# Moving one of four startup transposes from the matrix engine to VectorE, with a new block-0 schedule, a later bias transpose and a two-piece last split

## The chip, the cores and the metric

The kernel runs on one core of one Trainium2 chip. The metric is the time of one execution in device microseconds; lower is better. PE is the matrix engine (PEld its weight loads), DVE is VectorE, ACT is ScalarE, POOL is GpSimd and SP issues the DMAs. "Sub-tile j" is the j-th group of 128 tokens of a 512-token block; "f-tile" is a slice of 128 of the 3584 hidden features. In this kernel SBUF holds the tiles that the engines work on and PSUM the results of PE.

## The reference

```python
# B, S, D, F = 1, 2048, 1024, 3584, all bf16
def reference(x, w1, b1, w2, b2):
    y = _layernorm(x, axis=-1)                       # no scale, no shift, eps 1e-5
    h = _gelu(jnp.einsum("bsd,df->bsf", y, w1) + b1) # tanh approximation
    return jnp.einsum("bsf,fd->bsd", h, w2) + b2
```

## The kernel before

The tokens are taken in four blocks of 512 (four sub-tiles each). For every block PE computes `w1.T @ yT` per f-tile into one of four PSUM banks `pa`, ScalarE applies bias and GELU into `hT`, and then PE multiplies `hT` with `w2` into two banks `pb`, from which VectorE adds `b2` and writes the output tile. PE needs the normalised tokens transposed (`yT`).

For blocks 1 to 3 VectorE does that transpose in SBUF, far ahead of need. For block 0 nothing is ahead: PE transposes all four sub-tiles into PSUM (`pt`), ScalarE copies the first two to `yT`, VectorE the last two. So that PE can begin early, block 0 is computed in pieces, as sub-tiles become ready. The configuration says so:

```python
n_warm=12, n_fill=(2, 0, 0, 0),
# (first f-tile, end, first sub-tile, end)
sched0=((0, 2, 0, 1), (0, 2, 1, 2), (2, 4, 0, 2), (0, 4, 2, 3), (4, 8, 0, 3), (8, None, 0, 4), (0, 8, 3, 4)),
tpos=(0, 0, 5, 9),      # before which group PE transposes sub-tile j
edve=(2, 3),            # sub-tiles that VectorE copies out of PSUM
dve0=(("Sa", 0), ("Sb", 0), ("Sa", 1), ("Sb", 1), ("N", 0), ("N", 1), ("Sa", 2), ("Sb", 2),
      ("Sa", 3), ("N", 2), ("Sb", 3), ("E", 2), ("N", 3), ("E", 3)),   # VectorE's order in block 0
b1pos=0,                # PE transposes the bias row before the first group
last_split=(256, 128, 128),
```

`Sa` and `Sb` are statistics of the two halves of a sub-tile (they wait for its load), `N` the normalisation, `E` the copy from PSUM. The two ways to transpose are:

```python
def dve_transposes(t):                   # VectorE, SBUF to SBUF, blocks 1 to 3
    ...
    for si in range(4):
        for dj in range(4):              # 16 instructions of 32 x 256
            ...
            op("dve", lambda e, src=src, dst=dst: e.transpose(dst, src), ...)

def pe_transposes(j):                    # PE, block 0
    ...
    for dt in range(KD):                 # 8 of 128 x 128
        op("pe", lambda e, j=j, dt=dt: e.transpose(pt[tbank[j]][:, dt, :],
                                                   xs[j][:, dt * P:(dt + 1) * P], ident[:]), ...)

for b in range(NB):                      # PE's order
    for gi, (ft, j0, j1) in enumerate(groups[b]):
        if b == 0:
            for j in range(NJ):
                if tpos[j] == gi and j not in dtr0:
                    pe_transposes(j)
                    ...
            if b1pos == gi:
                pe_b1()
        pe_group(b, gi, ft, j0, j1)      # 8 matmuls of 128*(j1-j0) columns
    ...                                  # then the w2 matmuls of this block
```

## Time and profile before

| | before |
|---|---|
| median of the first 4 runs (later 13 runs) | 401.59 us (401.71 us) |
| span of the profiled run | 400.0 us |
| PE busy | 98% of the span |
| PE in the chain of work that ended last | 97% |
| 512-column matmul to the next | 215.8 ns |

The 215.8 ns are 10.79 us per 50 matmuls in the chain. The Trainium skill, "TensorE: Matmul & The Clock Gate", section Back-to-back issue gap, gives N/2.4 + 2.5 ns for warm matmuls, which is 215.8 ns for N = 512: this trace agrees. The kernel needs the equivalent of 1792 such matmuls, 386.7 us. What can be gained lies in the first 16 us, in the last 3 us, and in PE work that is no needed matmul.

Start of the kernel before, in the chain of waits (the chain that ended last, in order of time; columns: start in us, length in us, engine, tile, source line). Line 452 is PE's transposes, 471 the first matmul, 438 the bias transpose:

```profile
8.43 0.62 PE pt L452 x8
9.05 0.12 PE pb L438
9.17 2.93 PE pa L471 x40
12.10 0.45 PE pt L452 x8
12.55 2.30 PE pa L471 x32
14.85 0.45 PE pt L452 x8
15.29 5.65 PE pa L471 x40
...
397.65 0.29 DVE osb L341
```

The transposes of sub-tile 2 stand at 12.10 us and those of sub-tile 3 at 14.85 us. Each eight take 0.45 us and there is PE work directly before and after them, so they are on the critical path. The last line is the last output addition.

VectorE in the same stretch, in the timeline (start, length, line, operation, `[idle before, and what ended it]`):

```profile
13.66 0.55 DVE L311 TENSOR_SCALAR xs<-xs,mv,rs 128x1024 bf16<-128x1024 bf16 x1 [0.38 <-POOL rs L296]
15.33 0.69 DVE L346 COPY yT<-pt 128x1024 bf16<-128x1024 bf16 x1 [1.12 <-PE pt L452]
15.94 0.68 DVE L300 BATCH_NORM_STATS2 st<-xs 128x6 f32<-128x512 bf16 x1
...
20.63 7.18 DVE L328 STREAM_TRANSPOSE yT<-xs 32x256 bf16<-32x256 bf16 x16
```

The first line is sub-tile 3's normalisation, the second the copy of its transposed form out of PSUM. The last line is what the VectorE way of transposing one sub-tile costs: 7.18 us for 16 instructions, here in block 1.

The end of the kernel, in the timeline. The gap between the starts of two additions is the time of the 28 matmuls between them:

```profile
391.47 0.69 DVE L341 TENSOR_TENSOR osb<-pb,b_bc 128x512 bf16<-128x512 f32 x1 [5.35 <-PE pb L491]
...
394.52 0.42 DVE L341 TENSOR_TENSOR osb<-pb,b_bc 128x256 bf16<-128x256 f32 x1 [2.36 <-PE pb L491]
396.09 0.29 DVE L341 TENSOR_TENSOR osb<-pb,b_bc 128x128 bf16<-128x128 f32 x1 [1.14 <-PE pb L491]
397.65 0.29 DVE L341 TENSOR_TENSOR osb<-pb,b_bc 128x128 bf16<-128x128 f32 x1 [1.27 <-PE pb L491]
```

### The profile page before, as it was taken

What the parts mean: (1) busy time and instruction counts of PE and PEld (TensorE: products, weight loads), DVE (VectorE), ACT (ScalarE), POOL (GpSimd) and SP (SyncE); (2) the same over time, 40 slices, a digit from 0 to 9 for tenths busy, and PEclk for the clock granted to TensorE, in tenths of its full rate; (3) what the DMA queues carried; (4) which work ended last, traced back from release to release, by engine and by line L of the source; (5) the groups of instructions that cost most, each with busy time, mean ns of one, the idle gap of its engine ahead of it and who ended that gap; (6) DMA issues with size and microseconds to landing.
All of it is one profiled execution on the core that took longest, in us unless ns stands there. A gap on an engine that the chain in (4) does not pass through costs nothing.

```text
span 400.0 us, 4581 instructions
## 1 busy us (share of the span) xinstructions
PE 393.5 (98%) x1972; PEld 187.6 (47%) x2007; DVE 138.0 (35%) x292; ACT 83.9 (21%) x131; POOL 15.7 (4%) x41
## 2 busy tenths in 40 slices
PE   7999999999999999999999999999999999999997
PEld 3744464444444444444444444444444444444446
DVE  5699930110399940101159991001100000001101
ACT  3533450000033442000023344100003334400000
POOL 3211000000011000000010000000000000000000
DMA  8999940000000000000000000000000000000000
GB/s 245 369 387 386 387 147 13 28 13 26 28 0 2 0 1 2 26 13 28 24 15 2 0 0 2 0 28 26 13 28 13 0 2 0 0 15 26 15 26 27
DMA packets 17486, 23.62 MB, mean 59 GB/s; under 512 B 1339, under 2 KB 9787, under 8 KB 17467
## 3 DMA queue, kind: packets, MB, share of 16 engines
q1 hardware_dynamic: 17466, 23.34, 16.7%
q8 instruction: 15, 0.25, 0.3%
q14 instruction: 5, 0.03, 0.0%
HBM read 19.14 MB, written 4.19 MB: 58 GB/s over the span
## 4 chain that ended last, share of the span: by engine, by line
PE 97%; DMA 1%; DVE 1%; issue 1%; POOL 0%; SPq 0%
PE pa L471 48%; PE pb L491 48%; DMA xs<-in_x_dram 1%; PE pt L452 0%; SPq L252 0%; DVE st L300 0%; DVE st L304 0%; POOL rs L296 0%; DVE xs L311 0%; POOL ve L293 0%; DVE osb L341 0%; DVE mv L306 0%; PE pb L438 0%
## 5 line engine op out<-in xcount | busy, mean ns | idle before, releaser
L471 PE MATMUL pa<-yT,w_sb 128*128 128x512 bf16 (+3 forms) x992 | 194.1, 355 | 0.8
L491 PE MATMUL pb<-w_sb,hT 128*128 128x512 bf16 (+2 forms) x933 | 193.0, 366 | 1.0
L471 PEld LDWEIGHTS pa<-yT,w_sb 128*128 128x128 bf16 x1008 | 93.2, 98 | 100.8 <-DVE yT L346 0.2
L491 PEld LDWEIGHTS pb<-w_sb,hT 128*128 128x128 bf16 x952 | 90.8, 98 | 102.7
L415 ACT ACTIVATE hT<-pa,b_sb 128x512 bf16<-128x512 f32 (+3 forms) x126 | 80.3, 640 | 259.4 <-PE pa L471 258.5
L341 DVE TENSOR_TENSOR osb<-pb,b_bc 128x512 bf16<-128x512 f32 (+2 forms) x34 | 22.4, 660 | 248.3 <-PE pb L491 248.3
L328 DVE STREAM_TRANSPOSE yT<-xs 32x256 bf16<-32x256 bf16 x192 | 83.7, 436 | 2.9
L293 POOL TENSOR_SCALAR ve<-mv 128x1 f32<-128x1 f32 x16 | 5.3, 334 | 209.5 <-DVE mv L306 209.5
L300 DVE BATCH_NORM_STATS2 st<-xs 128x6 f32<-128x512 bf16 x16 | 11.0, 685 | 5.8 <-DMA xs<-in_x_dram 5.6
L304 DVE BATCH_NORM_STATS2 st<-xs 128x6 f32<-128x512 bf16 x16 | 10.8, 677 | 0.0
L296 POOL TENSOR_TENSOR rs<-ve,mhalf 128x1 f32<-128x1 f32 x16 | 9.1, 568 | 1.3
L311 DVE TENSOR_SCALAR xs<-xs,mv,rs 128x1024 bf16<-128x1024 bf16 x16 | 8.2, 513 | 1.3 <-POOL rs L296 1.2
L433 PE MATMUL pb<-zeros 128*128 128x512 bf16 x14 | 5.7, 584 | 1.4 <-POOL scr L283 1.4
L433 PEld LDWEIGHTS pb<-zeros 128*128 128x128 bf16 x14 | 1.8, 137 | 4.1 <-issue 2.8
L306 DVE BATCH_NORM_AGGREGATE mv<-st 128x2 f32<-128x12 f32 x16 | 3.3, 209 | 0.6
L452 PE MATMUL pt<-ident,xs 128*128 128x128 bf16 x32 | 2.5, 220 | 0.9 <-DVE xs L311 0.9
L403 ACT COPY yT<-pt 128x1024 bf16<-128x1024 bf16 x2 | 2.0, 1012 | 5.8 <-PE pt L452 5.8
L452 PEld LDWEIGHTS pt<-ident,xs 128*128 128x128 bf16 x32 | 1.9, 98 | 2.2 <-DVE xs L311 2.1
L346 DVE COPY yT<-pt 128x1024 bf16<-128x1024 bf16 x2 | 1.4, 690 | 1.1 <-PE pt L452 1.1
L399 ACT ACT_TABLE_LOAD x1 | 1.3, 1283 | 0.8 <-PEq L562 0.8
L282 POOL MEMSET zeros<- 128x512 bf16 x1 | 0.5, 524 | 0.3 <-POOLq L562 0.3
L286 POOL TENSOR_SCALAR_AFFINE_SELECT ident<-ones 128x128 bf16<-128x128 bf16 x1 | 0.3, 292 | 0.1
(11 smaller groups left out, 1.5 us busy)
## 6 DMA issues: line engine op xcount, KB each, us to landing
w_sb<-in_w_dram SPq DMA_DIRECT2D x9, 1024.0 KB, 14.4
w_sb<-in_w_dram SPq DMA_DIRECT2D x2, 2048.0 KB, 14.1
out_dram<-osb SPq DMA_DIRECT2D x31, 128.0 KB, 1.7
xs<-in_x_dram SPq DMA_DIRECT2D x15, 256.0 KB, 10.2
w_sb<-in_w_dram SPq DMA_DIRECT2D x2, 512.0 KB, 5.1
xs<-in_x_dram SPq DMA_DIRECT2D x2, 128.0 KB, 2.1
b_bc<-in_b_dram SPq DMA_DIRECT2D x1, 256.0 KB, 10.1
out_dram<-osb SPq DMA_DIRECT2D x1, 64.0 KB, 1.6
```

The costliest lines, as they stand in the source:

```text
L293: lambda e, t=t: e.tensor_scalar(ve[:, t:t + 1], mv[:, t, 1:2], EPS, None, ALU.add),
L296: lambda e, t=t: e.tensor_tensor(rs[:, t:t + 1], ve[:, t:t + 1], mhalf[:], ALU.pow),
L300: op("dve", lambda e, t=t: e.bn_stats(st[:, t, 0:6], xs[t][:, 0:512]), waits=[xev[(t, 0)]], meta=("bnst", 512))
L304: op("dve", lambda e, t=t: e.bn_stats(st[:, t, 6:12], xs[t][:, 512:1024]), waits=[xev[(t, 1)]], sig=("bs", t), ctr="bs", meta=("bnst", 512))
L311: lambda e, t=t: e.tensor_scalar(xs[t][:], xs[t][:], mv[:, t, 0:1], rs[:, t:t + 1], ALU.subtract, ALU.mult),
L328: op("dve", lambda e, src=src, dst=dst: e.transpose(dst, src), waits=waits if k == 0 else (), sig=("yT", t) if last else None, ctr="dt", m ...
L341: lambda e, slot=slot, gi=gi, c0=c0, c1=c1: e.tensor_tensor(osb[slot][:, c0:c1], pb[gi % NBK][:, 0:c1 - c0], b2_bc[:, c0:c1], ALU.add),
L415: lambda e, ft=ft, tok=tok, n=n, bank=bank: e.activation(hT[:, ft, tok], pa[bank][:, 0:n], ACT.Gelu_apprx_tanh, bias=b1_sb[:, ft:ft + 1], ...
L433: lambda e: e.matmul(pb[1][:], lhsT=zeros[:, 0:P], rhs=zeros[:], start=True, stop=True),
L452: lambda e, j=j, dt=dt: e.transpose(pt[tbank[j]][:, dt, :], xs[j][:, dt * P:(dt + 1) * P], ident[:]),
L471: lambda e, b=b, ft=ft, dt=dt, tok=tok, n=n, bank=bank: e.matmul(pa[bank][:, 0:n], lhsT=w1_sb[:, dt, ft * P:(ft + 1) * P], rhs=yT[b % 2][: ...
L491: lambda e, ft=ft, j=j, c0=c0, c1=c1, gi=gi: e.matmul(pb[gi % NBK][:, 0:c1 - c0], lhsT=hT[:, ft, j * P:(j + 1) * P], rhs=w2_sb[:, ft, c0:c ...
```

## The change

The intent is to take eight transposes off PE, which is always busy, and give them to VectorE, which is busy 35% of the time. VectorE is slower at it, so block 0 needs sub-tile 3 one f-tile later (9 instead of 8). Besides, the bias transpose moves behind two groups, the last output tile is split in two pieces instead of three, and the block's end loses the option that spared GpSimd its drain. The rest of the diff turns the configuration into constants and removes unused bookkeeping; the order and sizes of the loads stay.

```diff
-    sched0=((0, 2, 0, 1), (0, 2, 1, 2), (2, 4, 0, 2), (0, 4, 2, 3), (4, 8, 0, 3), (8, None, 0, 4),
-            (0, 8, 3, 4)),
-    tpos=(0, 0, 5, 9),
-    edve=(2, 3),
-    dtr0=(),
-    dve0=(... ("Sa", 3), ("N", 2), ("Sb", 3), ("E", 2), ("N", 3), ("E", 3)),
-    b1pos=0,
-    last_split=(256, 128, 128),
+SCHED0 = ((0, 2, 0, 1), (0, 2, 1, 2), (2, 4, 0, 2), (0, 4, 2, 3), (4, 9, 0, 3), (9, None, 0, 4),
+          (0, 9, 3, 4))
+TPOS = (0, 0, 5)
+B1POS = 2
+DVE0 = (... ("Sa", 3), ("N", 2), ("Sb", 3), ("E", 2), ("N", 3), ("D", 3))   # D: 16 VectorE transposes
+LAST_SPLIT = (384, 128)
 ...  (cut: constants in place of the configuration, bookkeeping)
-        block = es.enter_context(nc.Block(no_gpsimd_drain=True))
+        block = es.enter_context(nc.Block())
```

## The prediction

> **What bounds the kernel.** The matrix engine. The page gives PE 98% busy and the chain of waits is 97% PE. From 9 us to 397.65 us it is all but never idle: the waits view lists 0.9 us for normalised x and 1.4 us at the very start. A 512-column matmul follows the next at 215.8 ns (10.79 us per 50 in the chain), as the Trainium skill, "TensorE: Matmul & The Clock Gate", Back-to-back issue gap, gives with N/2.4 + 2.5 ns; 1792 such equivalents are 386.7 us of a 400.0 us span. Only the first 16 us, the last 3 us and PE work that is not a needed matmul can be saved.
>
> **What the change does, by parts.**
> 1. Eight PE transposes of sub-tile 3 go. In the chain they take 0.45 us (14.85 to 15.29), with no PE wait on either side. Saved: 0.45 us, all on the critical path.
> 2. In place of one 0.69 us copy from PSUM, VectorE does 16 transposes of 0.435 us: 7.18 us in block 1's timeline. The normalisation of sub-tile 3 starts at 13.66 us, so they should run from 14.24 to about 21.42 us. Block-0 work that needs sub-tile 3 starts one f-tile later (9 instead of 8): the PE has five 384-column groups of 1.30 us, to about 21.65 us. Slack only 0.1 to 0.2 us, but both sides hang on the same arrival of x sub-tile 3, so it should hold. I expect a wait of 0 to 0.1 us.
> 3. One 512-column group becomes 384 + 128: same columns, 8 more matmuls of about 2.5 ns fixed cost: +0.02 us.
> 4. The bias transpose (0.12 us in the chain) moves behind the two groups of sub-tile 0. Before, the PE waits about 0.27 us for sub-tile 1's copy on ScalarE (the weight load at 10.16 us was released by it), so the 0.12 us was hidden: saving about 0. The bias copy starts 0.1 us later; four PSUM banks cover it.
> 5. Last split 256+128+128 becomes 384+128: 28 fewer matmuls; 3.05 + 1.57 us become an estimated 4.55: -0.07 us. The last piece, its 0.29 us addition and its store stay.
> 6. At the block's end GpSimd gets a drain and the other engines' drains merge with a semaphore instruction. GpSimd is idle from about halfway. Estimated 0 to -0.05 us.
> 7. Block-1 layernorm on VectorE starts at about 21.4 instead of 15.9 us and ends near 58 instead of 54 us. The first output addition is wanted at about 65 us and block 1's yT at 107 us: nothing waits.
>
> Sum: -0.45 - 0.07 + 0.02 - 0.02 + up to 0.1 = about -0.5 us of 401.6, 0.12%. **Predicted 401.1 us, 8 in 10 between 400.6 and 401.7; faster by over 2%: 0.01; within 2%: 0.98; slower by over 2%: 0.01.**
>
> **What would show it.** (1) 24 PE transposes instead of 32; no transpose piece near 14.9 us in the chain. (2) In the VectorE timeline a 16-transpose run of 7.2 us right after the fourth normalisation, ending near 21.4 us; at most a small new PE wait for yT from the transpose line. (4) The first sub-tile-1 matmul stays near 10.2 us. (5) A 384-wide addition, its matmuls ending 4.55 us after the piece before. (7) No new wait of additions or block 1.
>
> **What would make it wrong.** VectorE transposes slower while DMA writes at 385 GB/s and PE reads the same tile, so that the first full-width group waits up to a microsecond: the gain vanishes. Weights of f-tiles 4 to 8 needed 0.45 us earlier and not landed. A drain on GpSimd that takes microseconds. Execution spread (401.27 to 402.02) exceeds the whole effect.

## The result, and the profile after

| | before | after |
|---|---|---|
| median | 401.71 us (401.27 to 402.19, 13 runs) | 401.47 us (401.05 to 402.20, 9 runs) |
| ratio | | 0.9996, interval 0.9986 to 1.0005 |
| span of the profiled run | 400.0 us | 399.5 us |
| end of sub-tile 2's PE transposes (chain) | 12.55 us | 12.67 us |
| start of the last addition (chain) | 397.65 us | 397.28 us |
| between these two | 385.10 us | 384.61 us |

A ratio is the mean time of one kernel's fast runs over that of the other's of the same rounds, so it is not quite the ratio of the medians quoted.

By the clock the two are the same within noise, as predicted; the medians differ by 0.24 us. The prediction's 401.1 us was 0.37 us too low, inside its range; 0.12 us of that lies in the base, as the prediction started from the 401.59 us of four runs and all thirteen have 401.71 us. The range also holds the 401.59 us of no change at all, so lying in it shows little by itself. The result's list of runs holds a tenth fast run of after, 400.65 us, which the nine of its median leave out; with it the median would be 401.38 us. The trace sees more than the clock can: counted from the end of sub-tile 2's transposes, the rest of the kernel is 385.10 - 384.61 = 0.49 us shorter.

The chain after the change, at the same place (line 412 is PE's transposes, 429 the first matmul, 374 ScalarE's copy of sub-tile 1):

```profile
8.56 0.64 PE pt L412 x8
9.19 0.02 issue
9.21 1.02 ACT yT L374
10.24 0.05 issue
10.28 1.94 PE pa L429 x24
12.22 0.45 PE pt L412 x8
12.67 9.25 PE pa L429 x80
...
397.28 0.29 DVE osb L336
```

There is no transpose piece near 14.9 us, and after 12.67 us the list of waits names no further wait of PE. The bias transpose has left the chain: at this place in this run PE waits for ScalarE's copy of sub-tile 1, which is what covered the bias transpose before.

VectorE after the change:

```profile
13.32 0.55 DVE L303 TENSOR_SCALAR xs<-xs,mv,rs 128x1024 bf16<-128x1024 bf16 x1
13.90 7.18 DVE L319 STREAM_TRANSPOSE yT<-xs 32x256 bf16<-32x256 bf16 x16
21.11 0.69 DVE L292 BATCH_NORM_STATS2 st<-xs 128x6 f32<-128x512 bf16 x1
```

The 16 transposes run at once after the normalisation, take the same 7.18 us as in block 1, and end at 21.08 us. The loads run at 376 GB/s meanwhile, and ran at 387 GB/s during those of block 1 in before; the 16 that start at 208.09 us in before, when the loads are over (8 GB/s from 200 to 220 us), take 7.18 us too. The list of waits names no PE wait for them.

And the end:

```profile
391.17 0.69 DVE L336 TENSOR_TENSOR osb<-pb,b_bc 128x512 bf16<-128x512 f32 x1 [5.35 <-PE pb L448]
...
395.72 0.56 DVE L336 TENSOR_TENSOR osb<-pb,b_bc 128x384 bf16<-128x384 f32 x1 [3.86 <-PE pb L448]
397.28 0.29 DVE L336 TENSOR_TENSOR osb<-pb,b_bc 128x128 bf16<-128x128 f32 x1 [1.01 <-PE pb L448]
```

The 384-column piece takes 395.72 - 391.17 = 4.55 us, against 396.09 - 391.47 = 4.62 us for the 256 and the 128 before.

Two questions stayed. Is the 0.49 us really the sum of the named parts? And why did the clock show only half of it: did something give it back, or is it noise?

### The profile page after: what moved, and what is told of

Same layout as the page of the kernel before. It is cut to its first block, busy times and chain, and to the rows that moved or that the text cites. A ratio compares the mean times of both kernels' runs of the same rounds, so it can differ in the third digit from the quotient of the medians.

```text
span 399.5 us, 4536 instructions
## 1 busy us (share of the span) xinstructions
PE 393.1 (98%) x1944; PEld 186.1 (47%) x1979; DVE 144.2 (36%) x306; ACT 84.3 (21%) x132; POOL 15.6 (4%) x41
## 4 chain that ended last, share of the span: by engine, by line
PE 97%; DMA 1%; issue 1%; DVE 1%; ACT 0%; POOL 0%; SPq 0%
PE pb L448 48%; PE pa L429 48%; DMA xs<-in_x_dram 1%; PE pt L412 0%; ACT yT L374 0%; SPq L245 0%; DVE st L292 0%; DVE st L296 0%; POOL rs L288 0%; DVE xs L303 0%; POOL ve L285 0%; DVE osb L336 0%; DVE mv L298 0%
## 5 line engine op out<-in xcount | busy, mean ns | idle before, releaser
L448 PEld LDWEIGHTS pb<-w_sb,hT 128*128 128x128 bf16 x924 | 89.3, 98 | 104.2
L319 DVE STREAM_TRANSPOSE yT<-xs 32x256 bf16<-32x256 bf16 x208 | 90.7, 436 | 3.1
```

Source lines behind the costliest of these rows:

```text
L448: lambda e, ft=ft, j=j, c0=c0, c1=c1, gi=gi: e.matmul(pb[gi % NBK][:, 0:c1 - c0], lhsT=hT[:, ft, j * P:(j + 1) * P], rhs=w2_sb[:, ft, c0:c ...
```

## The experiments

The yardstick below is the one of the table: from the end of sub-tile 2's PE transposes to the start of the last addition, called *the stream*. It leaves out the start, which differs from execution to execution. The start is told by when these transposes end, called *the start*. Both are read from the chain or, where the chain ran through another engine, from PE's timeline.

| run | start, us | last addition, us | stream, us | median, this / before, us | ratio (interval) |
|---|---|---|---|---|---|
| before | 12.55 | 397.65 | 385.10 | | |
| after | 12.67 | 397.28 | 384.61 | 401.47 / 401.71 | 0.9996 (0.9986 to 1.0005) |
| e1 after again | 12.08 | 396.69 | 384.61 | 401.07 / 401.55 | 0.9984 (0.9969 to 0.9999) |
| e2 after, old block end | 12.14 | 396.75 | 384.61 | 401.05 / 401.55 | 0.9987 (0.9969 to 1.0005) |
| e3 before, new block end | 13.04 | 398.14 | 385.10 | 401.28 / 401.55 | 0.9987 (0.9971 to 1.0004) |
| e4 before, transposes moved | 12.81 | 397.49 | 384.68 | 401.23 / 401.55 | 0.9987 (0.9972 to 1.0002) |
| e5 after, split at 8 | 12.07 | 397.52 | 385.45 | 402.14 / 401.32 | 1.0015 (1.0000 to 1.0031) |
| e6 before, 128 more transposes | 12.17 | 404.42 | 392.25 | 408.55 / 401.32 | 1.0175 (1.0161 to 1.0188) |
| e7 after, VectorE reordered, split at 11 | 12.49 | 397.13 | 384.64 | 400.91 / 401.32 | 0.9987 (0.9974 to 0.9999) |
| e8 after, VectorE reordered | 12.31 | 397.23 | 384.92 | 400.98 / 401.32 | 0.9989 (0.9976 to 1.0001) |
| e9 after, bias late, old place | 13.07 | 397.68 | 384.61 | 401.88 / 401.49 | 1.0005 (0.9990 to 1.0020) |
| e10 after, bias late, new place | 12.25 | 396.86 | 384.61 | 401.15 / 401.49 | 0.9989 (0.9972 to 1.0005) |
| e11 after, old last split | 12.08 | 396.76 | 384.68 | 400.95 (one run) / 401.49 | |
| e12 after, old block end, again | 12.09 | 396.70 | 384.61 | 401.12 / 401.42 | 0.9992 (0.9978 to 1.0006) |

The stream repeats to the hundredth of a microsecond between executions that have the same PE work, while the start moves by a microsecond. That is what makes effects of 0.07 us readable here, where the clock's interval is some 0.4 to 0.7 us to either side.

This yardstick was chosen after the first four runs. The expectations of e1 and e4 name another, from the second x tile's first statistics to the last addition, which takes in part of the loads: it is 392.53 us in before, 392.04 in after and 392.14 in e1 (recorded there as "about 390.0"), but 393.72 in e3, which has the same PE work as before, and 392.91 in e4. By it the expectation of e4 was missed; e3 shows that it does not measure the change.

### e1, e2, e3: is the gain given back at the block's end?

The profiled run of after took 401.67 us with a span of 399.5 us, before took 401.86 us with 400.0 us: 0.3 us more outside of the span. The drain on GpSimd, new at the block's end, was the suspect (theory B); theory A is that only noise hides the gain.

e1 is the changed kernel unaltered.

> The changed kernel once more. Theory A (the change takes 0.5 us of PE work out of the span and the medians differ by less only because executions spread over 1 us): median 0.3 to 0.7 us below the kernel before of the same rounds; in the trace the last addition again starts about 390.0 us after the second x tile's first statistics (392.53 before, 392.04 in the profile of after). Theory B (the span gains 0.5 us but the tail outside of the span gives 0.2 to 0.3 us back, because of the drain on GpSimd): median only 0.1 to 0.3 us below, and time minus span again near 2.1 us against 1.86 us before.

e2 takes the drain from the changed kernel, e3 gives it to the kernel before:

```diff
# e2
-        block = es.enter_context(nc.Block())
+        block = es.enter_context(nc.Block(no_gpsimd_drain=True))
# e3: the reverse, in the kernel before
```

> The changed kernel with the old block end (no drain on GpSimd). Theory A: the same as e1 within 0.1 us, time minus span unchanged. Theory B: 0.2 to 0.3 us faster than e1, so about 0.5 us below the kernel before, and time minus span back near 1.86 us.

> The kernel before with only the new block end (drain on GpSimd, the other engines' drain merged). Theory A: same as the kernel before within 0.1 us. Theory B: 0.2 to 0.3 us slower than the kernel before, the span itself unchanged.

e1 came out 0.48 us below before and e2 0.50 us: no gain from taking the drain away that the clock can see. It cannot see much: e3, which saves no PE work, has the same ratio, 0.9987, as e2 and e4, so the ratios do not show the saving. What decides is time minus span. e1 has 2.08 us and e2 1.90 us in the median, as theory B expects, but e2's six runs scatter from 1.67 to 2.14 us; and e3, the drain alone, has 1.83 us against 1.85 us for before, where B asked for 0.2 to 0.3 us more. So the drain alone costs no time that shows, and theory B in this form falls. In the span the new block end even saves a little: from the start of the last addition to the end of the span it is 2.22 us in e1 and in after, 2.23 us in e3, but 2.32 us in before and 2.30 us in e2. The trace shows why it can: there the separate drain and semaphore instruction of SP at the end are one.

The time outside of the span is taken up again under e12.

### e4: the move of the transposes alone

```diff
# in the kernel before
-    sched0=(... (4, 8, 0, 3), (8, None, 0, 4), (0, 8, 3, 4)),   edve=(2, 3), dtr0=(),   ... ("E", 3)),
+    sched0=(... (4, 9, 0, 3), (9, None, 0, 4), (0, 9, 3, 4)),   edve=(2,), dtr0=(3,),   ... ("D", 3)),
```

> The kernel before with only the move of sub-tile 3's transposes to VectorE and the 9-instead-of-8 schedule. Theory A: 0.43 us less from the second x tile's first statistics to the last addition (392.53 us before), no PE wait for the VectorE transposes, median 0.2 to 0.7 us below before. Rival C (VectorE transposes come too late and PE waits): interval shortened by less than 0.2 us and a wait of PE for yT from the transpose line of some tenths of a us near 21 us.

The chain, with the end of sub-tile 2's transposes and the last addition:

```profile
12.19 0.62 PE pt L452 x8
12.81 11.19 PE pa L471 x89
...
397.49 0.29 DVE osb L341
```

The stream is 384.68 us: 385.10 - 384.68 = 0.42 us shorter, and there is no PE wait for VectorE's transposes. The move alone is thus 0.42 of the 0.49 us. In this run x sub-tile 3 came late and the transposes ended only at 21.74 us (started 14.56 us, 7.18 us long); PE still did not wait. Rival C (they come too late and PE waits) falls.

### e5: is the new schedule needed for it?

```diff
# in the changed kernel
-SCHED0 = (... (4, 9, 0, 3), (9, None, 0, 4), (0, 9, 3, 4))
+SCHED0 = (... (4, 8, 0, 3), (8, None, 0, 4), (0, 8, 3, 4))
```

> The changed kernel with the block-0 schedule split at f-tile 8 as before, sub-tile 3 still transposed on VectorE. Theory A (VectorE's 7.18 us of transposes just fit behind five 384-column groups): with four of them the PE is ready 1.30 us earlier, the transposes are not, so a PE wait for yT of 0.4 to 1.2 us near 20 to 21 us; from the end of sub-tile 2's PE transposes to the last addition 385.0 to 385.8 us instead of 384.61, which is about or worse than the kernel before (385.10). Rival C (the retune of the schedule is idle): no such wait, 384.6 us.

The stream became 385.45 us, 0.84 us longer than with the split at 9, and longer than before. The list of waits of e5 names the reason (columns: engine, tile and line, what it waited for, us in total, times, longest):

```profile
PE pa L429 <- DVE yT L319: 0.7, 1, 0.7
```

Line 319 is the VectorE transposes. The timeline shows PE starting on the first full-width group only as they end:

```profile
13.46 7.18 DVE L319 STREAM_TRANSPOSE yT<-xs 32x256 bf16<-32x256 bf16 x16
...
20.70 9.67 PE L429 MATMUL pa<-yT,w_sb 128*128 128x512 bf16 x44 [0.68 <-DVE yT L319]
```

The idle time listed is 0.68 us, the stream grew by 0.84. The other 0.16 us fits how the idle time is counted, from the modelled end of the matmul before: at the start of this stream the next matmul starts at 11.91 us, 0.16 us before the modelled end of the transposes at 12.07 us.

By the clock the kernel is just slower than before (402.14 against 401.32 us, ratio 1.0015, 1.0000 to 1.0031). The one f-tile more is 1.30 us of PE work; in this run 0.84 us of it was needed. The move and the split at 9 belong together: the move without the later split costs more than it brings.

### e6: what one PE transpose costs

```diff
# in the kernel before, pe_transposes
-        for dt in range(KD):
+        reps = 17 if j == 3 else 1
+        for k in range(reps * KD):
+            dt = k % KD
```

The waits stand at the first and the signal at the last of them, and the result is unchanged.

> The kernel before with sub-tile 3's eight PE transposes done 17 times over (128 more, same result). If one costs 56 ns in the stream as the chain says: 7.15 us more, time about 408.7 us, ratio about 1.018. If a PE transpose costs the 220 ns that the page gives as its mean duration: 28 us more, about 430 us.

The stream grew by 392.25 - 385.10 = 7.15 us for 128 transposes, 55.9 ns each, and the median by 7.2 us. In the chain all 136 stand in one piece:

```profile
12.17 2.30 PE pa L473 x32
14.47 7.59 PE pt L454 x136
22.06 2.07 PE pa L473 x18
...
404.42 0.29 DVE osb L341
```

So the eight that the change removed were worth 8 x 55.9 = 447 ns. The profile page's group of PE transposes, in before, shows a mean of 220 ns; the Trainium skill, "Perfetto Trace Analysis", section Tensor Engine Instruction, says that PE's end times are estimated from size plus a delay rather than observed. This run agrees: spacing, not the mean length, is the cost.

### e7, e8: is it VectorE's queue order that makes the start vary?

In e3 and e4 sub-tile 2's normalisation stood behind sub-tile 3's first statistics, which waited for x sub-tile 3 until 11.23 and 10.99 us, and PE idled 0.35 and 0.63 us. Theory D was that this order makes the start vary; rival E that the first loads alone do.

```diff
# e7, in the changed kernel; with SCHED0 split at 11 instead of 9
-        ("Sa", 3), ("N", 2), ("Sb", 3), ("E", 2), ("N", 3), ("D", 3))
+        ("N", 2), ("E", 2), ("Sa", 3), ("Sb", 3), ("N", 3), ("D", 3))
# e8, split left at 9
+        ("N", 2), ("Sa", 3), ("Sb", 3), ("E", 2), ("N", 3), ("D", 3))
```

> The changed kernel with VectorE's queue reordered: sub-tile 2 is normalised and copied out of PSUM before sub-tile 3's first statistics, which wait for a load (split at f-tile 11, as sub-tile 3 then comes about 1 us later). Theory D (runs differ because the normalisation of sub-tile 2 stands in VectorE's queue behind statistics that wait for x sub-tile 3): the PE's transposes of sub-tile 2 end at 11.6 to 12.0 us from the span's start instead of 12.1 to 13.0 us, span medians 0.2 to 0.6 us below the changed kernel's 399.0, no new PE wait for sub-tile 3. Rival E (the landing of the first x tiles alone sets it): no gain, median again near 401.1 to 401.5 us.

> The changed kernel with sub-tile 2's normalisation alone put before sub-tile 3's first statistics. Theory D: transposes of sub-tile 2 earlier in runs in which x sub-tile 3 lands late, but its copy out of PSUM still behind sub-tile 3's statistics, so PE waits for that copy instead: 0 to 0.3 us gained. Rival E: no gain. The VectorE transposes then end later by up to 0.7 us, and a PE wait for them of 0 to 0.5 us may appear.

Both miss their main expectation. The start in e7 was 12.49 us, not 11.6 to 12.0 us, and the median span is 399.0 us, the same as e1's. The chain of e7 shows why this run started late: x sub-tile 1 landed at 5.06 us (4.55 us or earlier in e1), and statistics, normalisation, PE transpose and ScalarE's copy of sub-tile 1 follow one another from there to 10.05 us. Here, as rival E has it, sub-tile 1's load set the start. The chains of e3 and e4 run as theory D says, from x sub-tile 3's load through its statistics to sub-tile 2's normalisation; that the new order helps in such an execution no run shows, and it is no general gain. e8's stream is 0.31 us longer than after's, and PE waits for sub-tile 2's copy there (0.22 us idle in its timeline), as expected. Against before, the ratios of e7 and e8 (0.9987 and 0.9989) are about those of e1 and e2, so neither is shown to beat the changed kernel.

### e9, e10: what the bias transpose's new place is for

In e3's profile PE waited at the old place: the list of waits names the bias row's load. (The wait did not set the start there: the chain of e3 runs through x sub-tile 3, which landed at 11.20 us.)

```profile
PE pb L438 <- DMA b1row<-in_b_dram: 0.8, 1, 0.8
```

To see this on purpose, the load of the bias row was put one load later, with the transpose in the old place (e9) and in the new one (e10):

```diff
# both, in the changed kernel
-LOADS = (... ("x", 2), ("b1",), ("w1", 2, 4), ("x", 3), ...
+LOADS = (... ("x", 2), ("w1", 2, 4), ("b1",), ("x", 3), ...
# e9 only
-B1POS = 2
+B1POS = 0
```

> The changed kernel with the bias row's load issued one load later (behind the second piece of w1) and the bias transpose put back in front of the first matmul group. Theory F (the old place makes the first matmul wait for the bias row when it lands late): PE waits 0.5 to 1.5 us for the bias row, the first matmul of sub-tile 0 starts at 9.0 to 10.5 us instead of 8.3 to 9.0, the transposes of sub-tile 2 end 0.2 to 1.0 us later than in e10, median 0.1 to 0.8 us over e10. If the bias transpose is hidden whatever the landing: no difference from e10.

> The same late load of the bias row, with the bias transpose in its new place behind the two groups of sub-tile 0. Theory F: first matmul at 8.3 to 9.0 us, the wait for the bias row at most 0.5 us and overlapped with the wait for sub-tile 1's copy; time as the changed kernel's, 401.0 to 401.5 us.

The row landed at about the same time in both, 9.63 and 9.67 us. In the chain of e9 the whole start hangs on it:

```profile
3.73 5.90 DMA b1row<-in_b_dram
9.63 0.05 issue
9.67 0.18 PE pb L463
9.86 2.77 PE pa L429 x40
12.62 0.45 PE pt L412 x8
```

In e10 PE had meanwhile done the two groups of sub-tile 0, and the same transposes of sub-tile 2 stand 0.81 us earlier:

```profile
3.74 5.93 DMA b1row<-in_b_dram
9.67 0.05 issue
9.72 0.18 PE pb L463
9.90 1.90 PE pa L429 x24
11.81 0.45 PE pt L412 x8
```

The median spans differ by the same 0.8 us (399.85 and 399.05 us), the median times by 0.73 us. Theory F holds: the new place saves nothing when the row is early and up to 0.8 us, in this test, when it is late.

### e11: the last split alone

```diff
# in the changed kernel
-LAST_SPLIT = (384, 128)
+LAST_SPLIT = (256, 128, 128)
```

> The changed kernel with the old last split 256+128+128. 28 more matmuls of 2.5 ns fixed cost: from the end of sub-tile 2's PE transposes to the last addition 384.68 us against 384.61, and the last two 128-column pieces and the 256 one end 3.05 + 1.57 us after the piece before.

The stream is 384.68 us, 0.07 us longer than after's, as expected. Together with e4 the account closes: 0.42 + 0.07 = 0.49 us.

### e12: the time outside of the span

> The changed kernel without the drain on GpSimd once more, for the part of the reported time that lies outside of the profiled span. It was 1.83 us (median) for the kernel before of the last call, 2.03 to 2.13 us for kernels with the new block end in it, and 1.90 us in e2, with a wide spread (1.67 to 2.14). If the drain is its cause: median 1.8 to 1.9 us here, and span minus last addition 0.1 us longer than with the drain (2.32 against 2.22 us), so at most 0.1 us net. If it is not: median 2.0 to 2.1 us again.

The median of time minus span is 2.06 us here, against 1.83 us for the kernel before. So taking the drain away does not remove the difference; in e2 it seemed to (1.90 us), and this repeat did not bear that out. Over all calls this difference is 1.81 to 1.85 us for the kernel before, 1.83, 1.88 and 1.81 us for the variants of it (e3, e4, e6), and 1.90 to 2.13 us for the changed kernel and its variants. Against before of the same call that is 0.05 (e2) to 0.3 us, mostly about 0.2 us, of the changed kernel's gain that is given back where the profile does not look. Putting the bias transpose back (e9, 2.03 us) does not remove it either; the drain alone (e3) does not bring it and the moved transposes alone (e4) hardly. What does is open; the old last split had only one run (1.95 us).

## Why the prediction was right or wrong, point by point

1. *"Saved: 0.45 us, all on the critical path."* Right. e6 gives 0.447 us for eight transposes, and e4 shows 0.42 us net of the 8 extra matmuls.
2. *Slack of 0.1 to 0.2 us, wait of 0 to 0.1 us.* The wait was 0 in every profile with this order and the split at 9. The transposes ended at 21.08 us in the profile of after, earlier than the 21.42 us expected, because x sub-tile 3 landed earlier; in e4 they ended at 21.74 us. The slack differs from run to run. In the instruction records of the traces the first full-width matmul starts 0.15 us after the last of the 16 transposes ends in e1 (21.17 and 21.01 us) and in e4 (21.89 and 21.74 us), which is the size predicted, and 0.62 us after it in e2; e5 puts it at about 1.30 - 0.84 = 0.46 us in its run (an estimate from those two). The smallest slack seen is thus 0.15 us, and the split at 9 has no f-tile to spare. The fear that VectorE's transposes slow down under load was unfounded: 7.18 us with loads at 376 GB/s and without.
3. *+0.02 us for splitting a group.* In accord with e4 (0.42 instead of 0.447 us) and with e7, where two more split f-tiles added 0.03 us.
4. *The bias transpose: "saving about 0".* Right for the executions in which the row has landed by then, as in the profile of before, and incomplete: I had looked at one trace. When the row lands late, the old place holds up the first matmul (0.8 us of waiting in e3), and in e9 against e10 this cost 0.8 us of span.
5. *-0.07 us for the last split.* Right to the hundredth (e11).
6. *Block end: 0 to -0.05 us.* In the span it is about -0.09 us (2.22 instead of 2.32 us after the last addition starts; e1 against e2 has 0.08), slightly more than I allowed; by the clock no effect can be seen (e1 against e2, e3 against before).
7. *Nothing later waits.* Right: the rest of PE's stream is as long as the sum of its parts says.

The sum, about -0.5 us, was right for the traced stream, -0.49 us, and not by luck: e4, e6 and e11 find its large terms at the sizes predicted. By the clock the changed kernel was 0.24 us below before in the first comparison and 0.48 us in the second. A term missing from the sum is the roughly 0.2 us that the changed kernel takes more outside of the span, which no view of the profile could have told me beforehand and whose cause stays open. Another part can lie in the start: it ended between 12.07 and 13.07 us in these profiles, twice the whole effect. I had named the spread of executions as larger than the effect, and it is.

## What to carry to other kernels

When one engine is always busy, move its work to an idle one even if that one needs sixteen times as long, but find out what the result is waited for and give the busy engine enough other work first: here 7.18 us of VectorE work bought 0.42 us of PE work, and with one f-tile too few of cover it became a loss. Read a small effect from a stretch of the trace that starts behind the noise of the loads and ends with the last useful instruction; it repeated to 0.01 us where the clock could hardly tell 0.5 us. And look at the start of more than one execution before you call a wait hidden: which load comes late differs from run to run.

## What the Trainium skill lacked or had wrong

- "TensorE: Matmul & The Clock Gate", section Back-to-back issue gap: it says that in real streams of weight load and matmul the sustained spacing is about 131 ns for N = 512 and 81 ns for N = 128. Here it is 215.8 ns and, in the last 128-column piece of before, 1.56 us / 28 = 55.7 ns: the formula N/2.4 + 2.5 ns, which that section keeps for isolated matmuls, is what this stream follows.
- The same page, Part 4: PE-mode transpose, gives about 275 ns for a 128x128 transpose in a kernel's context and says the full clock does not engage for it. The 275 ns is a length, for which the trace has 220 ns here; in the stream one transpose costs 55.9 ns (e6), as much as a matmul of that size, and the clock granted in the 7.5 us of transposes of e6 was 1.00.
- "VectorE: DVE Perf Modes", section The three transpose paths, gives 311 ns for VectorE on 128x128 but no cost for a full transpose put together from 32x32 blocks. Here eight full 128x128 blocks take 7.18 us, 0.90 us each.
- "Runtime: NRT & Kernel Launch", section The ~15µs preamble/postamble breakdown, lists what stands around a kernel, 9 to 15 us in total, and a gap of about 6.2 us, the same for all kernels, between a profile's total and the runtime's time. It has nothing on the part of the reported device time that lies outside of the profiled span here, which is about 2 us and differs between kernels: 1.81 to 1.85 us for the kernel before, 1.90 to 2.13 us for the changed one and its variants.
